# Soft-MoE dispatch sums as a seventh column of the slot product, and e replicated by TensorE

## The chip, the cores and the metric

The kernel runs on one core of a Trainium2 chip. The metric is device time in microseconds (us) of one execution; lower is better. The engines are TensorE (PE; its weight loads are shown apart as PEld), VectorE (DVE), ScalarE (ACT), GpSimd (POOL) and SyncE (SP), each with its own queue of instructions, taken in order.

## The reference, cut to what matters

Soft-capped attention for 8 batches, 12 heads, 448 tokens, head size 64, and then a soft mixture of experts over all 3584 tokens of 768 features, with 32 slots (8 experts of 4):

```python
scores = cap * np.tanh((q @ k.T) / np.sqrt(64) / cap)      # cap = 30
attn = softmax(scores)
x = (attn @ v)                                             # (3584, 768) after the heads are joined
logits = x @ phi                                           # (3584, 32)
d = np.exp(logits - logits.max(0)); d /= d.sum(0) + 1e-09  # dispatch: over the tokens
slot_input = d.T @ x                                       # (32, 768)
for e in range(8):
    h = np.maximum(slot_input[e] @ w1[e], 0.0)
    slot_out[e] = h @ w2[e]
c = np.exp(logits - logits.max(1)); c /= c.sum(1) + 1e-09  # combine: over the slots
return c @ slot_out
```

So one matrix e = exp(logits) serves twice. Summed over the tokens it is the divisor of the dispatch (one number for each slot); turned over, it is the weight of the combine.

## The kernel before, in words

**Stages.** The attention takes the time up to 245 us, then come the experts on the 32 slots (two layers), then the combine and the stores of 11 MB.

**Attention.** Two pairs of heads make a quad (24 quads Q, 48 pairs pr). A score tile is 128 keys by 448 queries, seven of them to a pair, 336 in all. Six tiles make a chunk j (56 chunks); seven chunks (PER) are a batch b. In these texts k is j modulo 7. For each chunk PE makes the scores in two halves of three tiles (`qk_chunk`, L315, into two PSUM buffers `sc`), ACT takes tanh of each half (`tanh_chunk`, L324), and one chunk later exp (`exp_chunk`, L328). Of 33 chunks some tiles are taken off ACT: `SHARED` says how many (78 in all, one to three of a chunk), and `poly_exp` computes their exp on DVE in eight operations, numbered 0 to 7: L560, L562, L563, L564, L565, L566, L567, L568. Each operation works on all the tiles that were taken of the chunk at once. Two chunks after a pair's last tile PE multiplies with v (`pv_first`, `pv_tail`, `pv_rest`, L586; a column of ones in `vbd` gives the divisor) and DVE divides (`norm`: reciprocal L593, product `xq` L596). GpSimd copies v into `vbd` (`vcast`, L285), after `pv_rest` has read the old one, and issues the loads of q, k and the weights.

**Turning.** PE transposes q and k of a quad (`transp`, L275) and the attention's result (`x_transp`, L634 and L639), always into one PSUM bank, tag T of pool psT, which has a single buffer; DVE copies it out (L277, L648). The next use of T waits for that copy. T also serves `logits` (L653, L657), `slot_sums`, `e_norm`, `e_transp` and `e_sums`.

**Around e.** For each batch: `logits` fills `lps` with tokens on partitions in four groups of 128 (the last of 64) and 32 slots; `e_exp` has ACT write E (L673); `e_rep` has GpSimd write e4, four copies of E side by side (L679, 128x512); `slot_sums` multiplies x by E on PE (L719, L725) into `slps`, six columns of 32, and DVE adds them to `slacc` (L734); `e_norm` multiplies e4 by a column of ones into one column, the sum over the tokens, four times along the partitions, which DVE adds to `zacc` (L687, L691); `e_transp` turns e4 with four transposes (L698), and DVE copies the result to ET4 or ETl (L699). There the 32 slots stand four times along the partitions, as layer 2 leaves its results.

**Order.** Each engine takes its work in the order in which the loop over j emits it: tanh of the first half, slot m, tanh of the second half, slot e, exp of the chunk before, `pv_first`, slot a, `pv_tail`, `qk_chunk` for the first half of the next chunk, slot b, `pv_rest` (with slot r inside), slot c, `qk_chunk` for its second half, slot d. A slot has a part ahead (`<c`) and one behind (`>c`). The table `WHEN` puts each job of a batch into a slot, counted in chunks from the batch's start: for example `'x1': (8, 'c')`, the transposes of the batch's second quad; `k1` to `k3` and `q1` to `q3` are the transposes of k and q of three quads, `lg`, `ee`, `ss`, `et`, `en`, `es` the steps around e. The table `POLY` puts each DVE operation (chunk, number) into a slot. `FILL`, `LATE` and `spare` place matmuls without use between.

**After the attention.** The last two pairs are worked off by hand (`TAILSEQ`), then the last batch's e, its slot sums and the last column sums (`z_last`, L961 and L965), and `rz`, one over `zacc`, is made; ACT's relu of layer 1 multiplies by it (L1047). During the stores the last two batches' e are turned (`e_transp(B - 1)`, `e_rep(B - 2)`, `e_transp(B - 2)`), with one e4 buffer for both.

Of the kernel before, what the change touches and what calls it, by code (L numbers as in the profile page):

```python
# [9 lines left out]
F32 = mybir.dt.float32  # L10
# [8 lines left out]
P = 128  # L19
HP = 64  # L20
# [17 lines left out]
def kernel(  # L38
# [47 lines left out]
    half1 = consts.tile([P, 1], BF16, name="half1")  # L86
    pool.memset(half1, 0.0)
    pool.memset(half1[0:HP, :], 1.0)
# [6 lines left out]
    slacc = consts.tile([P, NJ, NS], F32, name="slacc")  # L95
    consts.tile([P, 192], BF16, name="pad")
# [233 lines left out]
    def exp_chunk(j):  # L330
# [11 lines left out]
            (3, '>c'): ((3, 3),),  # L342
            (3, '>d'): ((3, 4),),
            (4, '>a'): ((3, 5), (3, 6), (3, 7), (4, 0)),
            (4, '>c'): ((4, 1),),
            (4, '>d'): ((4, 2),),
            (5, 'e'): ((4, 3),),
            (5, '>b'): ((4, 4),),
            (5, '<c'): ((4, 5),),
# [7 lines left out]
            (7, '<c'): ((7, 2),),  # L357
            (7, '>c'): ((7, 3),),
            (7, '>d'): ((7, 4),),
            (8, '>b'): ((7, 5),),  # L360
            (8, '<c'): ((7, 6),),
            (9, 'e'): ((9, 0),),
            (9, '>a'): ((7, 7),),
# [5 lines left out]
            (10, '>d'): ((9, 6), (9, 7)),  # L369
            (11, '>a'): ((11, 0), (11, 1)),  # L370
            (11, '>b'): ((11, 2),),
# [5 lines left out]
            (12, '>c'): ((12, 2),),  # L377
            (13, '>a'): ((12, 3),),
# [4 lines left out]
            (14, '<c'): ((14, 2),),  # L383
            (14, '>c'): ((14, 3),),
            (14, '>d'): ((14, 4),),
            (15, '>b'): ((14, 5),),
            (15, '<c'): ((14, 6),),
            (16, 'e'): ((16, 0),),
            (16, '>a'): ((14, 7),),
# [5 lines left out]
            (17, '>d'): ((16, 6), (16, 7)),  # L395
            (18, '>a'): ((18, 0), (18, 1)),
            (18, '>b'): ((18, 2),),
# [5 lines left out]
            (19, '>c'): ((19, 2),),  # L403
            (20, '>a'): ((19, 3),),
# [4 lines left out]
            (21, '<c'): ((21, 2),),  # L409
            (21, '>c'): ((21, 3),),  # L410
            (21, '>d'): ((21, 4),),
            (22, '>b'): ((21, 5),),
            (22, '<c'): ((21, 6),),
            (23, 'e'): ((23, 0),),
            (23, '>a'): ((21, 7),),
# [5 lines left out]
            (24, '>d'): ((23, 6), (23, 7)),  # L421
            (25, '>a'): ((25, 0), (25, 1)),
            (25, '>b'): ((25, 2),),
# [5 lines left out]
            (26, '>c'): ((26, 2),),  # L429
            (27, '>a'): ((26, 3),),  # L430
# [24 lines left out]
            (33, '>c'): ((33, 2),),  # L455
            (34, '>a'): ((33, 3),),
# [4 lines left out]
            (35, '<c'): ((35, 2),),  # L461
            (35, '>c'): ((35, 3),),
            (35, '>d'): ((35, 4),),
            (36, '>b'): ((35, 5),),
            (36, '<c'): ((35, 6),),
            (37, 'e'): ((37, 0),),
            (37, '>a'): ((35, 7),),
# [5 lines left out]
            (38, '>d'): ((37, 6), (37, 7)),  # L473
            (39, '>a'): ((39, 0), (39, 1)),
            (39, '>b'): ((39, 2),),
# [5 lines left out]
            (40, '>c'): ((40, 2),),  # L481
            (41, '>a'): ((40, 3),),
# [4 lines left out]
            (42, '<c'): ((42, 2),),  # L487
            (42, '>c'): ((42, 3),),
            (42, '>d'): ((42, 4),),
            (43, '>b'): ((42, 5),),  # L490
            (43, '<c'): ((42, 6),),
            (44, 'e'): ((44, 0),),
            (44, '>a'): ((42, 7),),
# [5 lines left out]
            (45, '>d'): ((44, 6), (44, 7)),  # L499
            (46, '>a'): ((46, 0), (46, 1)),  # L500
            (46, '>b'): ((46, 2),),
            (46, '<c'): ((46, 3),),
            (46, '>d'): ((46, 4), (46, 5)),
            (47, 'e'): ((47, 0), (46, 6)),
# [6 lines left out]
            (48, '>b'): ((47, 6),),  # L511
            (48, '<c'): ((47, 7),),
            (48, '>d'): ((48, 1), (48, 2)),
            (49, '>a'): ((48, 3), (48, 4), (49, 0)),
            (49, '<c'): ((48, 5),),
            (49, '>c'): ((48, 6),),
            (49, '>d'): ((49, 1), (49, 2), (49, 3)),
            (50, '>a'): ((48, 7),),
            (50, '>b'): ((49, 4),),
            (50, '>d'): ((49, 5), (49, 6)),  # L520
            (51, 'e'): ((51, 0),),
            (51, '>a'): ((51, 1), (49, 7), (51, 2)),
            (51, '<c'): ((51, 3),),
            (51, '>d'): ((51, 4),),
            (52, 'e'): ((51, 5),),
            (52, '>a'): ((52, 0),),
            (52, '>b'): ((51, 6), (52, 1)),
            (52, '<c'): ((52, 2),),
            (52, '>c'): ((51, 7),),
# [139 lines left out]
    es, e4s = {}, {}  # L669

    def e_exp(b):
        es[b] = consts.tile([P, NG, NS], BF16, name="E", tag="E", bufs=2)
        act.activation(es[b], lps.pop(b), ACT.Exp)  # L673
        e_rep(b)

    def e_rep(b):

        e4s[b] = consts.tile([P, NG, 4 * NS], BF16, name="e4", tag="e4", bufs=1)
        pool.tensor_copy(e4s[b].rearrange("p g (a s) -> p g a s", a=4),  # L679
                         es[b].unsqueeze(2).to_broadcast([P, NG, 4, NS]))  # L680
# [86 lines left out]
    WHEN = {'k1': (-1, 'd'), 'q1': (0, 'a'), 'v1': (3, 'c'), 'k2': (2, 'b'), 'q2': (2, 'd'), 'v2': (7, 'b'), 'k3': (4, 'b'), 'q3': (5, 'b'), 'v3': (11, 'c'), 'x0': (5, 'a'), 'x1': (8, 'c'), 'x2': (10, 'b'), 'lg': (10, 'd'), 'ee': (11, 'm'), 'ss': (11, 'c'), 'et': (13, 'a'), 'en': (14, 'c'), 'es': (15, 'a')}  # L767

    for b in range(B):
        j, p = b * PER, 6 * b  # L770

        def when(nm):
            return j + WHEN[nm][0], WHEN[nm][1]

# [16 lines left out]
        if b < B - 1:  # L791
            at(*when("lg"), logits, b)
            at(*when("ee"), e_exp, b)
            at(*when("ss"), slot_sums, b)
            if b < B - 2:
                at(*when("et"), e_transp, b)
                at(*when("en"), e_norm, b)
            if b % 2:
                at(*when("es"), e_sums, b // 2)
# [155 lines left out]
    zl = bank([P, 1], name="zps")  # L955

    def z_last(b):
        for g in range(NG):
            n = P if g < NF else HP
            if b < bl:  # L960
                pe.matmul(zl, e4s[b][0:n, g, :], ones[0:n, 0:1], start=(g == 0), stop=False,  # L961
                          skip_group_check=True)
                continue
            for a in range(4):
                pe.matmul(zl[32 * a:32 * a + NS, :], es[b][:, g, :],  # L965
                          ones[:, 0:1] if g < NF else half1, start=False, stop=(g == NG - 1),
                          skip_group_check=True)
# [11 lines left out]
    z_last(bl - 1)  # L979
# [16 lines left out]
    e_rep(bl)  # L996
    z_last(bl)
# [4 lines left out]
    dve.tensor_tensor(zacc, zl, zacc, op=ALU.add)  # L1002
# [204 lines left out]
```

## Time and profile before

| | us |
|---|---|
| median of three runs (lowest, highest) | 293.06 (292.88, 293.4) |
| the profiled execution, its own time | 293.05 |
| its span, first to last instruction | 291.3 |
| busy: PE, DVE, ACT, POOL | 254.9, 241.9, 256.7, 138.8 |
| ACT's last exp of the attention ends | 245.1 |
| first store of the output is issued | 259.5 |

The mean granted clock of TensorE is 0.978. Times in the views are microseconds from the first instruction, and those called mean or from the trace's rows are of this one execution. A row of the timeline gives the start, the time taken, engine, line, operation, what it writes and reads, shapes, the number of instructions merged into it, and in brackets the engine's idle time before it and who ended that. A row of the waits gives who waited for whom, the sum, how often, and the longest.

### The profile page before, as it was taken

The page shows a single profiled execution, that of the slowest core. Times are in us where ns is not written, and L with a number is a line of the kernel's source. Part 1 is how long each engine was busy: PE and PEld are TensorE (multiplying, and loading weights), DVE is VectorE, ACT ScalarE, POOL GpSimd, SP SyncE. Part 2 cuts the span into 40 slices and gives each one's busy share as a digit, 9 for nine tenths or more (in the row PEclk, how much of TensorE's full clock was granted, in tenths as well). Part 3 has the DMA queues.
Part 4 walks back from the last instruction along what each step waited for, and adds up shares of the span by engine and source line. Part 5 has one row for each costly group of instructions (what it writes and reads, how often), then busy time and mean ns, then how long its engine had stood idle before and what let it go on. Part 6 is the DMA issues. An engine that isn't in the chain of part 4 may idle for free.

```text
span 291.3 us, 10806 instructions
## 1 busy us (share of the span) xinstructions
PE 254.9 (88%) x4728; PEld 172.8 (59%) x4728; DVE 241.9 (83%) x506; ACT 256.7 (88%) x211; POOL 138.8 (48%) x200
## 2 busy tenths in 40 slices
PE   8898789989998999899889998999899899998720
PEld 6655466757675767576657675767576668542400
DVE  3727899999999999999999999999999986247740
ACT  4999999999999999999989999999999997237720
POOL 4492645774666567555745656565553220300000
PEclk9999999999999999999999999999999999999965
DMA  7999999999999999999999999999999467979995
GB/s 242 242 192 205 207 183 218 213 206 217 229 224 181 209 234 231 200 207 230 215 196 199 222 218 201 215 228 226 206 184 228 122 227 254 409 290 377 411 423 234
DMA packets 58478, 68.11 MB, mean 234 GB/s; under 512 B 4160, under 2 KB 54592, under 8 KB 58432
## 3 DMA queue, kind: packets, MB, share of 16 engines
q0 software_dynamic: 42448, 35.31, 78.2%
q1 hardware_dynamic: 15696, 31.89, 31.3%
q8 instruction: 37, 0.61, 0.8%
q10 hardware_dynamic: 288, 0.23, 0.2%
q14 instruction: 9, 0.07, 0.1%
HBM read 91.72 MB, written 19.27 MB: 381 GB/s over the span
## 4 chain that ended last, share of the span: by engine, by line
DVE 47%; PE 33%; ACT 8%; DMA 4%; POOL 2%; issue 2%; DVEq 0%; ACTq 0%
PE pv L586 11%; DVE xq L596 8%; PE sc L315 5%; DVE ex L567 5%; DVE xp L566 4%; DVE xT L648 4%; ACT ex L328 3%; DVE xp L564 3%; DVE xf L562 3%; ACT ex L324 3%; DVE ex L560 3%; DVE ex L568 3%; PE pv L616 3%; DVE xp L563 3%; DVE qT L277 3%; DVE kT L277 2%
## 5 line engine op out<-in xcount | busy, mean ns | idle before, releaser
L324 ACT ACTIVATE ex<-sc 128x1344 f16<-128x1344 f32 (+1 forms) x113 | 142.1, 1318 | 2.5 <-PE sc L315 2.4
L328 ACT ACTIVATE ex<-ex 128x2688 bf16<-128x2688 f16 (+5 forms) x58 | 110.2, 1904 | 0.1
L586 PE MATMUL pv<-vbd,ex 128*128 128x130 bf16 (+1 forms) x1610 | 95.1, 211 | 7.6 <-POOL vbd L285 4.7
L586 PEld LDWEIGHTS <-ex 128*128 128x128 bf16 (+1 forms) x1680 | 75.7, 101 | 36.0 <-PE sc L315 7.7
L315 PE MATMUL sc<-qT,kT 64*64 64x448 bf16 x672 | 70.5, 359 | 1.1 <-ACT ex L324 0.7
L285 POOL CAST vbd<-vraw 64x896 bf16<-64x896 f32 x46 | 44.2, 960 | 45.9 <-PE pv L586 30.2
L596 DVE TENSOR_TENSOR xq<-pv,rec 128x448 bf16<-128x448 f32 x46 | 28.7, 624 | 1.6
L315 PEld LDWEIGHTS <-kT 64*64 64x64 bf16 x672 | 23.4, 105 | 6.6 <-issue 5.1
L293 POOL MEMSET vbd<- 64x1 bf16 x22 | 4.0, 180 | 46.3 <-PE pv L586 46.3
L117 POOL DMA_DIRECT2D w1b<-in_moe_w_dram x32 | 24.9, 781 | 0.0
L566 DVE TENSOR_TENSOR xp<-xp,xf 128x1344 f16<-128x1344 f16 (+2 forms) x33 | 23.6, 715 | 0.9
L564 DVE TENSOR_TENSOR xp<-xp,xf 128x1344 f16<-128x1344 f16 (+2 forms) x33 | 23.9, 723 | 0.2
L567 DVE TENSOR_TENSOR ex<-ex,xp 128x1344 uint16<-128x1344 uint16 (+2 forms) x33 | 23.2, 704 | 0.4
L679 POOL COPY e<-E 128x512 bf16<-128x512 bf16 x9 | 6.2, 693 | 36.4 <-PE eps L698 19.9
L616 PE MATMUL pv<-ones 128*128 128x57 bf16 x474 | 18.6, 188 | 0.0
L185 POOL DMA_DIRECT2D qb<-in_q_dram x22 | 16.8, 765 | 3.1 <-DMA kraw<-in_k_dram 3.1
L277 DVE COPY kT<-kps 128x896 bf16<-128x896 bf16 x23 | 14.2, 617 | 4.5 <-PE kps L275 4.3
L275 PE MATMUL qps<-ident,qb 128*64 128x128 bf16 x308 | 12.8, 222 | 5.4 <-DVE xT L648 5.3
L563 DVE TENSOR_SCALAR xp<-xf 128x1344 f16<-128x1344 uint16 (+2 forms) x33 | 16.6, 504 | 0.2
L275 PEld LDWEIGHTS <-qb 128*64 128x64 bf16 x308 | 10.1, 109 | 10.8 <-issue 10.5
L560 DVE TENSOR_SCALAR ex<-ex 128x1344 uint16<-128x1344 f16 (+2 forms) x33 | 16.4, 498 | 0.0
L616 PEld LDWEIGHTS <-ones 128*128 128x128 bf16 x474 | 16.2, 96 | 0.0
(135 smaller groups left out, 361.8 us busy)
## 6 DMA issues: line engine op xcount, KB each, us to landing
w1b<-in_moe_w_dram POOLq DMA_DIRECT2D x32, 384.0 KB, 8.4
vraw<-in_v_dram SPq DMA_DIRECT2D x44, 224.0 KB, 6.1
w2d<-in_moe_w_dram POOLq DMA_DIRECT2D x21, 384.0 KB, 8.5
w2t<-w2d SPq DMA_DIRECT2D x21, 384.0 KB, 7.0
out_dram<-ob SPq DMA_DIRECT2D x7, 768.0 KB, 8.0
qb<-in_q_dram POOLq DMA_DIRECT2D x22, 224.0 KB, 7.5
kb<-in_k_dram POOLq DMA_DIRECT2D x22, 224.0 KB, 6.0
w2b<-in_moe_w_dram POOLq DMA_DIRECT2D x11, 384.0 KB, 7.5
```

What stands on the lines that cost most here:

```text
L277: dve.tensor_copy(t, ps)
L285: pool.tensor_copy(vbds[Q % 2][r, :, :, c0:c0 + DH], raw[r])
L315: pe.matmul(sc[cs, u, 0:S], qkT["k", Q][r, c, cs], qkT["q", Q][r, :, cs], start=True, stop=True)
L324: act.activation(exs[j][:, half * CS + u0:half * CS + u1, :].bitcast(F16), sc[:, u0:u1, 0:S], ACT.Tanh, scale=qk_scale / cap)
L328: act.activation(exs[j][:, u0:u1, :], exs[j][:, u0:u1, :].bitcast(F16), ACT.Exp, scale=cap)
L563: lambda: dve.tensor_scalar(p, f, c3, c2, ALU.mult, ALU.add),
L564: lambda: dve.tensor_tensor(p, p, f, op=ALU.mult),
L566: lambda: dve.tensor_tensor(p, p, f, op=ALU.mult),
L567: lambda: dve.tensor_tensor(y, y, p, op=ALU.add),
L586: pe.matmul(out_, exs[j][r, u, q0:q0 + (HP if tail else P)], v_, start=(c == 0 and g == gs[0] < NF), stop=(c == NT - 1), skip_group_check= ...
L596: dve.tensor_tensor(xq[Q][:, h, s0:s1, :], pv[:, 0:s1 - s0, 0:DH], rec.to_broadcast([P, s1 - s0, DH]), op=ALU.mult)
L616: pe.matmul(home, ones, ones[:, 0:512 - NT * W], start=False, stop=True, skip_group_check=True)
```

## The change

- `e_rep`, `e_norm` and `z_last` go, with e4 and half1. Nothing is copied by GpSimd for e any more.
- `slot_sums` gets a seventh column of 32 in `slps` and `slacc`: a new `z_mms` multiplies a 128x128 block of ones by E, four matmuls, so that each partition holds the sums of all 32 slots.
- At the end DVE adds the last batch's sums to it (`zsum`), multiplies by the identity read as four blocks of 32 (`zdiag`), and reduces each partition to its own slot's sum (`zacc`).
- `e_transp` does sixteen transposes of E's 32 columns, four for each group, each to 32 other partitions, in place of four of 128 columns of e4.
- `SHARED` takes two tiles of chunk 53 instead of one: 79 in all.
- `WHEN`: q1 goes from slot a to slot b of its chunk, x1 from (8, c) to (8, d), x2 from (10, b) to (10, a); `en` goes.
- `POLY` is written anew from chunk 3 on. Below are the rows of one round (chunks 28 to 34) and those of chunks 53 to 55.

```diff
-    slacc = consts.tile([P, NJ, NS], F32, name="slacc")
-    consts.tile([P, 192], BF16, name="pad")
+    slacc = consts.tile([P, NJ + 1, NS], F32, name="slacc")
+    zsum = consts.tile([P, NS], F32, name="zsum")
+    zdiag = consts.tile([P, 4, NS], F32, name="zdiag")
+    consts.tile([P, 336], BF16, name="pad")
...
             (28, '>b'): ((28, 1),),
-            (28, '<c'): ((28, 2),),
-            (28, '>c'): ((28, 3),),
+            (28, '>c'): ((28, 2), (28, 3)),
             (28, '>d'): ((28, 4),),
             (29, '>b'): ((28, 5),),
-            (29, '<c'): ((28, 6),),
-            (30, 'e'): ((30, 0),),
-            (30, '>a'): ((28, 7),),
+            (29, '>c'): ((28, 6),),
+            (29, '>d'): ((28, 7),),
+            (30, '>a'): ((30, 0),),
...
             (31, '>a'): ((30, 5),),
-            (31, '>d'): ((30, 6), (30, 7)),
-            (32, '>a'): ((32, 0), (32, 1)),
-            (32, '>b'): ((32, 2),),
+            (31, '>d'): ((30, 6),),
+            (32, 'e'): ((32, 0), (30, 7)),
+            (32, '>a'): ((32, 1), (32, 2)),
             (32, '<c'): ((32, 3),),
             (32, '>d'): ((32, 4), (32, 5)),
             (33, 'e'): ((32, 6),),
             (33, '>a'): ((32, 7), (33, 0)),
             (33, '>b'): ((33, 1),),
-            (33, '>c'): ((33, 2),),
-            (34, '>a'): ((33, 3),),
+            (33, '<c'): ((33, 2),),
+            (34, 'e'): ((33, 3),),
             (34, '>b'): ((33, 4), (33, 5)),
...
-            (53, 'e'): ((52, 4), (53, 0), (52, 5)),
-            (53, '>a'): ((52, 6),),
+            (53, 'e'): ((52, 4), (52, 5)),
+            (53, '>a'): ((53, 0), (52, 6)),
             (53, '>b'): ((52, 7), (53, 1)),
             (53, '<c'): ((53, 2), (53, 3)),
-            (53, '>c'): ((53, 4),),
-            (54, '>a'): ((53, 5), (53, 6)),
-            (54, '>c'): ((54, 0), (54, 1), (54, 2)),
-            (54, '>d'): ((53, 7),),
-            (55, 'e'): ((54, 3), (54, 4), (54, 5)),
+            (54, 'e'): ((53, 4),),
+            (54, '>b'): ((53, 5), (53, 6)),
+            (54, '<c'): ((54, 0),),
+            (54, '>c'): ((53, 7), (54, 1), (54, 2), (54, 3)),
+            (55, 'e'): ((54, 4), (54, 5)),
             (55, '>a'): ((54, 6), (54, 7))}
...
         act.activation(es[b], lps.pop(b), ACT.Exp)
-        e_rep(b)
-
-    def e_rep(b):
-
-        e4s[b] = consts.tile([P, NG, 4 * NS], BF16, name="e4", tag="e4", bufs=1)
-        pool.tensor_copy(e4s[b].rearrange("p g (a s) -> p g a s", a=4),
-                         es[b].unsqueeze(2).to_broadcast([P, NG, 4, NS]))
-
-    def e_norm(b):
-
-        ps = psT.tile([P, 1], F32, name="zps", tag="T")
+
+    def z_mms(b, dst, alone=False):
+
         for g in range(NG):
             r = slice(0, P if g < NF else HP)
-            pe.matmul(ps, e4s[b][r, g, :], ones[r, 0:1], start=(g == 0), stop=(g == NG - 1))
-        if b == 0:
-            dve.tensor_copy(zacc, ps)
-        else:
-            dve.tensor_tensor(zacc, ps, zacc, op=ALU.add)
+            pe.matmul(dst, ones[r, :], es[b][r, g, :], start=(alone and g == 0), stop=(g == NG - 1),
+                      skip_group_check=True)
...
         for g in range(NG):
             n = P if g < NF else HP
-            pe.transpose(ps[:, g * P:g * P + n], e4s[b][0:n, g, :], ident[0:n, 0:n])
+            for a in range(0, P, NS):
+                pe.transpose(ps[a:a + NS, g * P:g * P + n], es[b][0:n, g, :], ident[0:n, 0:n])
...
     def slot_sums(b):
-        ps = psT.tile([P, NJ, NS], F32, name="slps", tag="T")
+        ps = psT.tile([P, NJ + 1, NS], F32, name="slps", tag="T")
         slot_mms(b, ps, range(NG), range(NJ))
+        z_mms(b, ps[:, NJ, :])
...
-    e_rep(bl)
-    z_last(bl)
+    z_mms(bl, zl, True)
...
-    dve.tensor_tensor(zacc, zl, zacc, op=ALU.add)
+    dve.tensor_tensor(zsum, zl, slacc[:, NJ, :], op=ALU.add)
+    dve.tensor_tensor(zdiag, ident.rearrange("p (a s) -> p a s", s=NS),
+                      zsum.unsqueeze(1).to_broadcast([P, 4, NS]), op=ALU.mult)
+    dve.tensor_reduce(zacc, zdiag.rearrange("p a s -> p (a s)"), axis=mybir.AxisListType.X, op=ALU.add)
     dve.reciprocal(rz, zacc)
...
             e_transp(B - 1)
-            e_rep(B - 2)
```

More of the change, by code (lines that the diff above doesn't have):

```diff
@@ L341 @@
             (3, 'r'): ((3, 2),),
-            (3, '>c'): ((3, 3),),
+            (3, '<c'): ((3, 3),),
             (3, '>d'): ((3, 4),),
[L344 to L347, printed above, removed]
+            (4, '>a'): ((3, 5), (3, 6), (4, 0)),
+            (4, '>b'): ((3, 7),),
+            (4, '<c'): ((4, 1),),
+            (5, 'e'): ((4, 2), (4, 3)),
             (5, '>b'): ((4, 4),),
-            (5, '<c'): ((4, 5),),
+            (5, 'r'): ((4, 5),),
             (5, '>c'): ((4, 6),),
@@ L356 @@
             (7, '>b'): ((7, 1),),
-            (7, '<c'): ((7, 2),),
-            (7, '>c'): ((7, 3),),
+            (7, '>c'): ((7, 2), (7, 3)),
             (7, '>d'): ((7, 4),),
             (8, '>b'): ((7, 5),),
-            (8, '<c'): ((7, 6),),
-            (9, 'e'): ((9, 0),),
-            (9, '>a'): ((7, 7),),
+            (8, '>c'): ((7, 6),),
+            (8, '>d'): ((7, 7),),
+            (9, '>a'): ((9, 0),),
             (9, '>b'): ((9, 1),),
@@ L368 @@
             (10, '>a'): ((9, 5),),
-            (10, '>d'): ((9, 6), (9, 7)),
-            (11, '>a'): ((11, 0), (11, 1)),
-            (11, '>b'): ((11, 2),),
+            (10, '>d'): ((9, 6),),
+            (11, 'e'): ((11, 0), (9, 7)),
+            (11, '>a'): ((11, 1), (11, 2)),
             (11, '<c'): ((11, 3),),
@@ L382 @@
             (14, '>b'): ((14, 1),),
[L383 to L384 removed]
+            (14, '>c'): ((14, 2), (14, 3)),
             (14, '>d'): ((14, 4),),
             (15, '>b'): ((14, 5),),
[L387 to L389 removed]
+            (15, '>c'): ((14, 6),),
+            (15, '>d'): ((14, 7),),
+            (16, '>a'): ((16, 0),),
             (16, '>b'): ((16, 1),),
@@ L394 @@
             (17, '>a'): ((16, 5),),
-            (17, '>d'): ((16, 6), (16, 7)),
-            (18, '>a'): ((18, 0), (18, 1)),
-            (18, '>b'): ((18, 2),),
+            (17, '>d'): ((16, 6),),
+            (18, 'e'): ((18, 0), (16, 7)),
+            (18, '>a'): ((18, 1), (18, 2)),
             (18, '<c'): ((18, 3),),
@@ L420 @@
             (24, '>a'): ((23, 5),),
-            (24, '>d'): ((23, 6), (23, 7)),
-            (25, '>a'): ((25, 0), (25, 1)),
-            (25, '>b'): ((25, 2),),
+            (24, '>d'): ((23, 6),),
+            (25, 'e'): ((25, 0), (23, 7)),
+            (25, '>a'): ((25, 1), (25, 2)),
             (25, '<c'): ((25, 3),),
@@ L472 @@
             (38, '>a'): ((37, 5),),
-            (38, '>d'): ((37, 6), (37, 7)),
-            (39, '>a'): ((39, 0), (39, 1)),
-            (39, '>b'): ((39, 2),),
+            (38, '>d'): ((37, 6),),
+            (39, 'e'): ((39, 0), (37, 7)),
+            (39, '>a'): ((39, 1), (39, 2)),
             (39, '<c'): ((39, 3),),
@@ L954 @@
            psT.tile([P, 2 * P], BF16, name="xpl", tag="T")]
[L955 to L967, printed above, removed]
+    zl = bank([P, NS], name="zps")
     def x_last(s, copy):
@@ L978 @@
     x_last(0, act.copy)
-    z_last(bl - 1)
     busy(3)
```

90 lines of the change are left out of this document (41 added, 49 removed), and 2 rows, old and new, of the table SHARED.

## The prediction, made before the changed kernel ran

> **What bounds the kernel now.** First the table of stages (columns: busy time of PE, PEld, DVE, ACT and POOL with their instruction counts, granted clock, DMA share, GB/s).
>
> ```profile
> 30.00:60.00 30.00, 26.56 (x538) 18.53 (x538) 28.29 (x58) 30.00 (x24) 18.28 (x25) 1.00 1.15 203
> 150.00:180.00 30.00, 28.05 (x569) 19.76 (x568) 29.12 (x61) 29.11 (x22) 18.41 (x27) 1.00 1.22 211
> 210.00:240.00 30.00, 27.69 (x535) 19.27 (x535) 27.14 (x72) 29.89 (x23) 12.06 (x18) 1.00 0.90 187
> 245.00:250.00 5.00, 5.00 (x120) 3.72 (x121) 2.06 (x9) 1.39 (x5) 1.53 (x2) 1.00 1.01 350
> ```
>
> From 6.7 to 245.1 us ScalarE (ACT) is nearly never idle; VectorE (DVE) is close behind at 29.1 of 30. After 245.1 nothing is ACT's: 46.2 us of slot experts and stores, with DMA near 1.0, start from whatever ends the attention. So I ask how much ACT loses before 245.1, and what holds it up. Busy time hides small losses, since neighbouring ACT rows overlap by 0.1 to 0.2 us; I take start to start. A tanh of three tiles starts 1.171 after the last one, an exp of 6, 5, 4, 3 tiles takes 2.333, 1.960, 1.586, 1.213, an E 0.174. What exceeds these is lost: 3.9 us in all, 0.3 of it before 15 us, which the change does not touch. The rest, 3.6 us, lies in two places of the seven-chunk round (k is the chunk number j modulo 7): 1.41 us before E (k=4; 0.25, 0.35, 0.11, 0.28, 0.42 in batches 1 to 5) and 2.19 us before the second tanh of k=6 or, last, k=5 (0.10, 0.10, 0.07, 1.28, 0.12, 0.20, 0.32). The timeline of ACT shows three of them (start, duration, what was idle before):
>
> ```profile
> 111.74 0.28 ACT L673 ACTIVATE E<-lps 128x128 bf16<-128x128 f32 x1 [0.17 <-PE lps L657]
> 150.79 1.29 ACT L324 ACTIVATE ex<-sc 128x1344 f16<-128x1344 f32 x1 [1.14 <-PE sc L315]
> 200.45 0.28 ACT L673 ACTIVATE E<-lps 128x128 bf16<-128x128 f32 x1 [0.23 <-PE lps L657]
> ```
>
> Both wait for PE, but PE is not the cause. In an ordinary round the timeline reads:
>
> ```profile
> 171.81 0.80 POOL L679 COPY e<-E 128x512 bf16<-128x512 bf16 x1 [1.29 <-ACT E L673]
> 172.05 0.80 DVE L560 TENSOR_SCALAR ex<-ex 128x896 uint16<-128x896 f16 x1
> ...
> 177.42 0.62 DVE L648 COPY xT<-xps 128x896 bf16<-128x896 bf16 x1
> 178.09 0.58 PE L275 MATMUL qps<-ident,qb 128*64 128x128 bf16 x14 [0.77 <-DVE xT L648]
> ```
>
> DVE runs without a gap over 0.05 us from 161.7 to 186.8. Its copy of x0 (L648, k=5) comes 0.6 us after PE had finished the transposes; bank T has one buffer, so q3's transposes wait 0.77 us, then pv_rest, then the scores of k=6, which end 0.04 us before their tanh starts. DVE's lateness at k=5 is what ACT pays for at k=6. At 150.79 it is larger, because two DVE operations sat beside GpSimd's cast:
>
> ```profile
> 143.66 1.19 POOL L285 CAST vbd<-vraw 64x896 bf16<-64x896 f32 x1
> 143.85 1.26 DVE L563 TENSOR_SCALAR xp<-xf 128x896 f16<-128x896 uint16 x1
> ```
>
> L563 of two tiles takes 0.38 where GpSimd is idle.
>
> **The change, part by part.** *Copies of e.* Seven lie in the attention stage, 0.61 us each alone. Beside them DVE is slower: L568 of three tiles takes 0.50 alone and 0.73 on average in the six rows beside a copy; L560 of two tiles 0.39 and 0.80; L564 of one tile 0.38 and 0.80. That is 0.24 to 0.42 per batch, 2.8 us in all, and it falls at k=4, just ahead of the x0 copy. GpSimd's DMA issues can move into the freed place; beside one, L560 of two tiles lost 0.20. So the gain is between 0 and 0.42; I take 0.3. The Trainium skill (SBUF — State Buffer, Who interferes with whom) says that VectorE's two-port operations and GpSimd's hold a shared port pair exclusively, so that the second waits in full; the trace agrees with the row at 172.05, and by that rule the whole 0.42 would be gained, 0.8 us of DVE more over seven batches.
>
> *The old sums.* Four matmuls (0.27 of PE at k=0), one use of T and one DVE add of 0.14 go, in six batches. The new four matmuls have full weights and 32 columns like the 18 of L719 in 0.69 us: 4 x 0.038 = 0.15, now at k=4 ahead of the second scores of k=5, which stand 0.6 ahead of their tanh. The slot add grows from 192 to 224 columns: 0.35 x 32/192 is at most 0.06.
>
> *Transposes of e.* Four of 0.10 to 0.12 become sixteen with 32 columns of weights. Nearest rows: sixteen loads with one-column matmuls in that shape took 0.24 (L965), fourteen half-width transposes 0.58 (L275), so 0.25 to 0.66; I take 0.4 against 0.4 now. They stand in k=6, which has no pv and is padded with junk; the next scores are 0.98 ahead of ACT. The Trainium skill (TensorEngine Tiling, Key Properties) says that a change of tiling mode drains TensorE, which speaks against the new shape. PE's weight loads do show 0.36 of idle after the scores' 64x64 shape, and two such extra gaps would be 0.7; the sum would still not move, by the slacks that follow.
>
> *Moves on PE.* From k=6 to k=2 PE is late by its own work, not by waiting: second scores of k=1 are 0.70 ahead, of k=2 0.15 to 0.32. Here 0.27 goes with the old sums; x1 (0.6) moves behind the second scores of k=2 and q1 (0.58) behind the first of k=1. So even 0.8 more in k=6 leaves 0.2 everywhere. x2 moves ahead of k=4's first scores: it then waits for q2's copy until 167.32 and delays those scores by 0.45 of 1.6, but its own copy on DVE comes one L566 earlier (0.86), so that logits start when the second scores end, 0.3 sooner, and E is no longer late.
>
> *DVE's order.* At k=4 L563 moves ahead of k3's copy, away from the cast that cost 0.88 at 143.85. Under that cast then lie a PSUM copy, the reciprocal and xq, which no cast lengthened by over 0.02.
>
> *Tile 79.* ACT's exp of chunk 53 goes from 1.960 to 1.586, 0.37 less. DVE's eight operations grow from the one-tile row sum 2.74 to the two-tile sum 4.20: 1.45 more. DVE idles 0.25, 0.73 and 0.18 between 233.5 and 238.0, 1.16 in all, and the copy of e beside L564 (0.42) goes. I take the two as level: 0.
>
> *End.* Four matmuls go at 246.4 (PE waits for ACT there), sixteen become four at 248.9 beside the slT adds, which layer 1 waits for anyway. DVE's new multiply and reduce (128x128; the nearest rows are 0.15 to 0.35 each) put rz at about 250.1 instead of 249.6; its first use is at 252.24. The copies at 248.5 and 270.7 have nobody waiting beyond 0.2. So 0; with that cover gone it would be 0.5.
>
> **Sum**, against the profiled execution: span 291.3, time 293.05, which is the median of the runs shown. E's waits give 1.2 of 1.41; the small k=6 waits 0.5 of 0.59; the long one 1.2 of 1.28; the last 0.2 of 0.32; tile 79 nothing. From these 3.1 I take back 0.6: DVE works about 28.85 us per round now and 28.85 - 0.3 - 0.14 + 0.06, about 28.5, later, while ACT without waits needs 28.79 (14 x 1.171 + 3 x 2.333 + 1.586 + 3 x 1.213 + 0.174). With so little between them some 0.1 per round should remain. 293.05 - 2.5 = 290.5.
>
> **Rivals.** *ACT never waits* (chance 0.20): all 3.6 and the 0.37 of tile 79: 289.1. For it: DVE would have 0.3 to spare per round. Against it: one slow DVE operation uses that up. *PE takes over* (0.14): the sixteen transposes and drains cost more than the 0.98 of k=0 and every round gives back about 0.3 in seven: 290.5 + 2.1 = 292.6. For it: the slacks of 0.15 to 0.32 in k=2. Against it: q1, x1 and the old sums leave that stretch. *DVE sets the end* (0.14), the one on the other side: in chunks 53 to 55 the 1.45 us land on the x and xq copies that PE's tail waits for. If PE's transposes come as DVE is ready, the 1.16 of idle time is no cover; and if GpSimd's issues fill the freed places, the rounds gain nothing. Then 293.05 + 1.0 (between 0.3 and 1.45), 294.0. It decides from the point where xq of pair 45 ends after 242.6 less what the rounds gained.
>
> **How the numbers follow.** My forecast has 0.52. Measurement tells 0.2%, about 0.6 us, from no change: 292.5 to 293.6. The forecast and the first rival are faster, and a little of the second (0.04): 0.76. Same: the rest of the second, 0.10. Slower: 0.14. The range reaches from the first rival's 289.1 less 0.2 up to 293.2, over the second and its doubts; it leaves out the slower rival and the ends.
>
> **What would show it.** Right: no POOL row at L679; L560 and L568 at k=4 back at 0.39 and 0.50; PE's wait of qps for xT below 0.5 instead of 0.77; E starting 1.17 after its tanh; ACT's last exp ending near 242.6 instead of 245.1; the 46.2 after it unchanged. Wrong: ACT waits for sc at k=0 to k=2 (PE took over), xq of pair 45 later against ACT's last exp than now (DVE sets the end), or a longer stretch after the last exp. A single DVE operation of over 1 us beside a cast, as at 143.85, would also spoil it.

## The result, and the profile after

The changed kernel takes **290.72 us** (median of 22 runs, 289.8 to 294.21), the kernel before 293.01 beside it (22 runs, 292.6 to 295.52): a ratio of 0.9926, with an interval of 0.9903 to 0.995, or 2.2 us less. The forecast was 290.5.

The first profiled execution of the changed kernel took 293.29 us, mostly because TensorE's clock came up 8 us late in it, which is told in the last section; so the profile read here is that of a second execution of the same kernel (290.34 us, span 288.6), and the first is shown only where it says so.

The first part of the page, after (busy time, share of the span, instructions):

```profile
PE 253.2 (88%) x4812; PEld 172.0 (60%) x4812; DVE 239.5 (83%) x502; ACT 255.4 (89%) x211; POOL 134.7 (47%) x189
```

GpSimd has 4.1 us less than before, DVE 2.4 less, although DVE now does a 79th tile. The table of stages of the same execution, with the columns of the one that the prediction shows:

```profile
30.00:60.00 30.00, 26.66 (x545) 18.89 (x545) 28.16 (x59) 30.00 (x24) 18.10 (x24) 1.00 1.17 208
150.00:180.00 30.00, 28.06 (x578) 19.46 (x573) 29.00 (x58) 30.00 (x24) 18.03 (x26) 1.00 1.25 214
210.00:240.00 30.00, 27.50 (x558) 20.18 (x553) 27.28 (x74) 30.00 (x24) 9.29 (x14) 1.00 0.87 188
245.00:250.00 5.00, 5.00 (x107) 3.02 (x108) 1.74 (x8) 0.71 (x3) 1.81 (x1) 1.00 1.03 406
```

ACT is at 30.00 in all three stages of the attention; from 150 to 180 it was at 29.11. DVE is hardly less busy (29.00 against 29.12): its relief shows as an earlier start of what follows, not as idle time. ACT's timeline, the rows that answer to the three shown before:

```profile
110.99 0.71 ACT L665 ACTIVATE E<-lps 128x128 bf16<-128x128 f32 x1
198.11 0.34 ACT L665 ACTIVATE E<-lps 128x128 bf16<-128x128 f32 x1
207.44 1.29 ACT L323 ACTIVATE ex<-sc 128x1344 f16<-128x1344 f32 x1 [0.35 <-PE sc L314]
```

The E rows have no bracket any more: ACT is not idle before them (110.99 is 1.17 after the start of the tanh ahead, as in a row without loss). The row at 207.44 (second tanh of k=6, batch 6) is the largest wait that is left after 22 us, 0.53 from start to start. The whole account, by the prediction's measure (start to start beyond the pitches of tanh, exp and E, after 22 us):

| | before | after |
|---|---|---|
| ACT's first tanh starts | 6.72 | 6.87 |
| waits before E | 1.41 | 0.07 |
| waits for scores | 2.19 | 1.14 |
| ACT's last exp ends | 245.08 | 242.49 |
| from there to the end of the span | 46.20 | 46.07 |

The attention, from the first tanh to the end of the last exp, is 238.36 before and 235.62 after: 2.74 less, of which 2.39 are waits and 0.37 the exp of the 79th tile.

### The profile page after: what moved, and what is told of

Its sections match the earlier page's. It is cut to its first block, busy times and chain, and to the rows that moved or that the text cites. A ratio compares the mean times of both kernels' runs of the same rounds, so it can differ in the third digit from the quotient of the medians.

```text
span 291.5 us, 10965 instructions
## 1 busy us (share of the span) xinstructions
PE 256.1 (88%) x4812; PEld 173.3 (59%) x4812; DVE 239.7 (82%) x502; ACT 256.2 (88%) x211; POOL 134.7 (46%) x189
## 4 chain that ended last, share of the span: by engine, by line
DVE 41%; PE 37%; issue 8%; POOL 6%; DMA 3%; ACT 1%; DVEq 0%; ACTq 0%
PE pv L578 11%; DVE xq L588 8%; PE sc L314 7%; DVE xT L640 4%; DVE ex L559 4%; DVE xp L558 4%; DVE xp L556 3%; PE junk L811 3%; DVE qT L276 3%; DVE ex L560 2%; POOL vbd L284 2%; DVE xf L554 2%; DVE ex L552 2%; DVE rec L585 2%; PE so_ps L1040 2%
## 5 line engine op out<-in xcount | busy, mean ns | idle before, releaser
L314 PE MATMUL sc<-qT,kT 64*64 64x448 bf16 x672 | 73.0, 365 | 0.4 <-DVE qT L276 0.4
L284 POOL CAST vbd<-vraw 64x896 bf16<-64x896 f32 x46 | 45.7, 994 | 56.3 <-issue 25.6
L314 PEld LDWEIGHTS <-kT 64*64 64x64 bf16 x672 | 24.0, 106 | 6.3 <-issue 4.9
L116 POOL DMA_DIRECT2D w1b<-in_moe_w_dram x32 | 25.5, 797 | 0.0
L559 DVE TENSOR_TENSOR ex<-ex,xp 128x1344 uint16<-128x1344 uint16 (+2 forms) x33 | 24.1, 730 | 0.3
L276 DVE COPY qT<-qps 128x896 bf16<-128x896 bf16 x23 | 14.3, 621 | 3.1 <-PE qps L274 3.0
L184 POOL DMA_DIRECT2D kb<-in_k_dram x22 | 16.2, 735 | 0.5 <-PE kps L274 0.5
L560 DVE TENSOR_SCALAR ex<-ex 128x1344 uint16<-128x1344 uint16 (+2 forms) x33 | 16.1, 488 | 0.1
L555 DVE TENSOR_SCALAR xp<-xf 128x1344 f16<-128x1344 uint16 (+2 forms) x33 | 15.8, 479 | 0.3
```

Of the source, the lines that this page charges most:

```text
L184: pool.dma_start(out=t, in_=quad_ap(nm, Q))
L276: dve.tensor_copy(t, ps)
L284: pool.tensor_copy(vbds[Q % 2][r, :, :, c0:c0 + DH], raw[r])
L314: pe.matmul(sc[cs, u, 0:S], qkT["k", Q][r, c, cs], qkT["q", Q][r, :, cs], start=True, stop=True)
L559: lambda: dve.tensor_tensor(y, y, p, op=ALU.add),
```

## The experiments

Twelve runs were made: ten other kernels, and both kernels of the change once more. In each table row below, "E" and "scores" are ACT's waits after 22 us, and "attention" goes from the first tanh to the end of the last exp, all of one profiled execution; "time" is the median of 6 to 12 timed runs (of three in the first row), and the ratio is to the kernel before on the same chip (293.34, 293.24 or 293.47 there).

| kernel | E | scores | attention | tail | time | ratio, interval |
|---|---|---|---|---|---|---|
| before, as in the prediction | 1.41 | 2.19 | 238.36 | 46.20 | 293.06 | |
| before, once more | 1.84 | 2.20 | 238.67 | 46.18 | 293.13 | 0.9982 [0.9954, 1.001] |
| changed kernel | 0.07 | 1.14 | 235.62 | 46.07 | 290.39 | 0.989 [0.9842, 0.9938] |
| structure alone | 1.33 | 1.42 | 237.50 | 46.42 | 292.19 | 0.998 [0.9942, 1.0019] |
| order alone | 0.24 | 3.56 | 239.94 | 46.01 | 292.3 | 0.9968 [0.9931, 1.0005] |
| before, no copies | 1.60 | 0.83 | 237.15 | 46.41 | 291.83 | 0.9947 [0.9914, 0.998] |
| changed, copies back | 0.24 | 2.56 | 237.07 | 46.41 | 291.69 | 0.9956 [0.9916, 0.9995] |
| changed, 78 tiles | 0.26 | 1.62 | 236.62 | 46.38 | 291.52 | 0.9932 [0.9893, 0.9971] |
| changed, x2 back | 1.67 | 1.62 | 237.60 | 45.97 | 292.44 | 0.9978 [0.9946, 1.0011] |
| changed, no column sums | 0.04 | 1.35 | 235.65 | 46.00 | 290.6 | 0.99 [0.9859, 0.9941] |
| changed, L563 back | 0.10 | 1.69 | 236.10 | 45.58 | 290.18 | 0.9897 [0.9855, 0.994] |
| changed, q1 and x1 back | 0.21 | 2.05 | 238.28 | 46.76 | 290.7 | 0.991 [0.9879, 0.994] |
| changed, issues moved | 0.33 | 1.77 | 236.44 | 45.85 | 290.9 | 0.9933 [0.9896, 0.997] |

The profiled executions of "order alone" and "q1 and x1 back" had the late clock too; it costs the attention 1.7 us before 22 us, so their "attention" is not to be compared, their waits after 22 us are. Two executions of one kernel differ by 0.4 to 0.5 in the sum of these waits (3.60 and 4.04 before; 1.66 and 1.21 in the two profiles of the changed kernel), so smaller differences between rows are not read.

**The changed kernel once more**, with no edit.

> The changed kernel once more, unchanged, for a second profile. Its first profiled execution took 293.29 us while the median is 290.72, and loses 2.6 us before 22 us (first tanh at 7.60 instead of 6.72 us, 1.5 us of waits of the next tanhs), where the change alters nothing. Theory A, that this start is a chance of single executions: the new profile shows the first tanh near 6.7 us and about 290.5 us in all. Theory B, that the change slows the start for good: again 7.6 us and 293. Either way the waits of ACT after 22 us should again be about 1.7 us, none of them over 0.1 before E.

It gave 290.39 (289.76 to 292.89): the first profile was the untypical one. All readings of "after" above are from this run.

**Structure alone, and order alone.** The one has the seventh column, z_mms, the sixteen transposes and no copies, with the old tables; the other has the copies and the old sums with the new tables.

```diff
 # structure alone: the changed kernel with SHARED, POLY and WHEN of before
-    WHEN = {... 'q1': (0, 'b'), ... 'x1': (8, 'd'), 'x2': (10, 'a'), ...}
+    WHEN = {... 'q1': (0, 'a'), ... 'x1': (8, 'c'), 'x2': (10, 'b'), ...}
 # order alone: the kernel before with SHARED, POLY and WHEN of after, and
+    WHEN = {... 'en': (14, 'c'), ...}
```

> The new way of summing and replicating e, with the order (POLY, WHEN but for en) and the 78 tiles of before. Theory A, GpSimd's copies were what made DVE late: about 1.2 us of the 2.3 come from here, 291.8 us. Theory B, the copies' place is taken by GpSimd's DMA issues and the gain is the new order's: 292.8 us or more, with E's waits of 0.1 to 0.4 us at k=4 still there and the k=6 waits larger than before, because the column sums now stand ahead of the second scores of k=5.

> The old way of summing and replicating e (GpSimd's copies, e_norm at its old place), with the new order (POLY, q1, x1, x2) and 79 tiles. Theory A: x2 ahead of the first scores takes away E's waits (1.3 us) but DVE stays late beside the copies, 291.9 us. Theory B: the order does it all, 290.7 us, with no long wait at k=6. Theory C, the order only pays when the copies are gone: 293.0 us or more.

Each half alone gives about 1 us (292.19 and 292.3 against 293.34), and both intervals reach past 1; together they give 2.95 on that chip and 2.2 in the main measurement. Whether that is more than the sum of the halves, the intervals do not settle. The profiles show where each half stops. The structure alone cuts the waits for scores and leaves those before E (1.33). The order alone does the reverse; its profiled execution is the slowest of its twelve, so its waits may be larger than usual. The waits of ACT that its view lists show it (engine, line, waited for: sum, number, longest):

```profile
ACT ex L324 <- PE sc L315: 5.4, 9, 2.0
```

In the kernel before the same line reads 2.4 in two waits, 1.2 of them at the start; here 3.3 fall before 22 us, by the late clock, and 2.1 in five waits after it, where before has 1.1 in one. They fall at k=5 and k=6, and DVE stands behind them: ahead of the slot sums PE waits 2.5 us, in five rounds, for DVE's copy of k, where the kernel before and the changed one have 0.4 in one round. "Changed, copies back" below has the same order beside copies, with the seventh column; its waits for scores are 2.56 and its time is 1.5 below the kernel before. So the order does pay beside copies there, and the 3.56 here is the reading of one execution.

**Copies taken out of the kernel before, and put back into the changed one.**

```diff
 # before, no copies
     def e_rep(b):
+        if 0 < b < B - 1:
+            e4s[b] = e4s[0]
+            return
 # changed, copies back: at the end of e_exp, into a tile that nothing reads
+        pool.tensor_copy(e4.rearrange("p (g a s) -> p g a s", g=NG, a=4),
+                         es[b].unsqueeze(2).to_broadcast([P, NG, 4, NS]))
```

> The kernel before, with GpSimd's copies left out for batches 1 to 6 (e_norm and e_transp then read batch 0's e4, so the divisor and the combine weights of these batches are left out of the result). Theory A, each copy costs DVE 0.24 to 0.42 us that ACT pays for at k=6: 292.0 us, L560 of two tiles back at 0.39. Theory B, a DMA issue of GpSimd moves into the place: 292.8 to 293.0, with DVE operations beside L121 and L185 longer instead.

> The changed kernel with GpSimd's copy of E added again in each of the seven batches of the attention (written to a tile that nobody reads; DVE's last product of 128x128 takes part of that tile afterwards). Theory A, DVE's lateness by the copies is what the new structure takes away: waits of ACT after 22 us grow from 1.2 us to about 2.5, 291.5 us. Theory B, the copies cost nothing with the new order: 290.4 us.

Without copies the kernel before gets 1.5 us faster (291.83 against 293.34) and its waits for scores fall from 2.19 to 0.83; putting them back into the changed kernel costs 1.3 (291.69 against 290.39, two chips, so only roughly), with the waits up from 1.21 to 2.80. Both say that the copies are worth about 1.4 us, in the old order as in the new, with an interval of about 1 us to either side of each.

**78 tiles, and x2 back.**

```diff
 # 78 tiles
-              53: (2, 0),
+              53: (1, 0),
 # x2 back
-    'x2': (10, 'a')
+    'x2': (10, 'b')
```

> The changed kernel with one tile of chunk 53 on DVE instead of two, in the same slots. Theory A, ACT sets the end, as its last exp ends 2.6 us earlier and the 46.1 us after it are as before: 290.4 + 0.37 = 290.8 us. Theory B (the prediction's term of zero), DVE's 1.45 us more take back what ACT gains: 290.4 us. Theory C, DVE sets the end: below 290.2.

> The changed kernel with x2's transposes at (10, b) as before, behind the first scores of k=4. Theory A, x2's place alone makes E late: E's waits of 0.1 to 0.4 us come back in five batches, 1.3 us in all, 291.5 us. Theory B, ACT's waits only move between E and k=6 because DVE is the bound: E waits again, the waits at k=6 shrink by as much, 290.4 to 290.7 us.

With 78 tiles the attention is 1.00 longer (0.67 of it waits, the rest, 0.33, about the 0.37 of one tile's exp), and the tail is 0.3 longer, not shorter: DVE does not set the end with 79. With x2 in its old slot the waits before E are back, as the E rows of its ACT timeline say:

```profile
111.60 0.28 ACT L665 ACTIVATE E<-lps 128x128 bf16<-128x128 f32 x1 [0.16 <-PE lps L649]
...
199.49 0.28 ACT L665 ACTIVATE E<-lps 128x128 bf16<-128x128 f32 x1 [0.27 <-PE lps L649]
```

That is 1.67 before E against 0.07, and the attention is 1.98 longer, against 1.45 with the copies back: by these profiles the one letter in `WHEN` is worth rather more than all the copies, once those are gone.

**No column sums.**

```diff
-        z_mms(b, ps[:, NJ, :])
+        if b == 0:
+            z_mms(b, ps[:, NJ, :])
 ...
-            dve.tensor_tensor(slacc, ps, slacc, op=ALU.add)
+            dve.tensor_tensor(slacc[:, 0:NJ, :], ps[:, 0:NJ, :], slacc[:, 0:NJ, :], op=ALU.add)
```

> The changed kernel with the new matmuls for the column sums left out after batch 0, and six columns added instead of seven (the divisor misses batches 1 to 6). Theory A, these four matmuls stand ahead of the second scores of k=5 and are what keeps the waits at k=5 and k=6 alive (1.2 us after 22 us): those waits fall below 0.5 us, 289.7 us. Theory B, the waits come from DVE's x0 copy: unchanged, 290.3 us.

The attention is 235.65 against 235.62: leaving out the four matmuls at k=4 gains nothing. It does free PE (how much is told with PE's terms below), but the freed time turned into a longer wait for DVE's copy of x0, in the waits of PE of this kernel and, below it, of the changed one:

```profile
PE qps L274 <- DVE xT L640: 4.2, 7, 1.0
```

```profile
PE qps L274 <- DVE xT L640: 2.8, 7, 0.6
```

**The kernel before once more, and L563 back in the changed one.** The first asks whether the one long wait at 150.79 is an accident of one execution, the second whether the moved L563 is what removed it.

```diff
 # L563 back, for j = 11, 18, 25, 32, 39
-            (32, '>a'): ((32, 1), (32, 2)),
+            (32, '>a'): ((32, 1),),
+            (32, '>b'): ((32, 2),),
```

> The kernel before, for a second profile. The first one holds one long wait (1.28 us at 150.79) that I put down to L563 beside GpSimd's cast, and a second such pair at 228.8 (0.77 longer). Theory A, the pair is the order's fault and recurs: again waits of 3.6 us after 22 us, with DVE operations over 0.45 us longer beside L285. Theory B, it is a chance of single executions: about 2.3 us of waits, and a shorter span by as much than 291.3, unless other waits take its place.

> The changed kernel with operation 2 (L563) of the k=4 chunks 11, 18, 25, 32, 39 behind k3's copy again, as before. Theory A (the prediction), it then meets the cast of v and is up to 0.88 us longer in single rounds, and k=6 waits for it: 291.0 us or more. Theory B, no collision, since the cast waits for pv_rest: 290.4 us, and the earlier slps would even take away 0.1 us of waits at k=5.

It is no accident. In the second execution of the kernel before the timeline has the same rows at the same place, 0.18 later:

```profile
141.31 0.61 POOL L679 COPY e<-E 128x512 bf16<-128x512 bf16 x1 [0.83 <-ACT E L673]
142.60 1.49 POOL L121 DMA_DIRECT2D w2d<-in_moe_w_dram  x2
143.83 1.19 POOL L285 CAST vbd<-vraw 64x896 bf16<-64x896 f32 x1
144.03 1.26 DVE L563 TENSOR_SCALAR xp<-xf 128x896 f16<-128x896 uint16 x1
...
150.97 1.29 ACT L324 ACTIVATE ex<-sc 128x1344 f16<-128x1344 f32 x1 [1.15 <-PE sc L315]
```

GpSimd was busy from the copy up to the cast, with the load of k and two loads of weights between; DVE lost 0.37, 0.20 and 0.36 in three operations beside them. The cast starts 0.20 ahead of L563, which then ends 0.27 after it. With the copies gone L563 starts first. First the kernel before without copies, then the changed kernel with L563 back (there the same operation is called L560):

```profile
143.39 0.38 DVE L563 TENSOR_SCALAR xp<-xf 128x896 f16<-128x896 uint16 x1
143.45 1.11 POOL L285 CAST vbd<-vraw 64x896 bf16<-64x896 f32 x1 [1.16 <-PE pv L586]
```

```profile
142.40 0.38 DVE L560 TENSOR_SCALAR xp<-xf 128x896 f16<-128x896 uint16 x1
142.70 0.93 POOL L284 CAST vbd<-vraw 64x896 bf16<-64x896 f32 x1 [0.97 <-PE pv L583]
```

L563 starts first by 0.06 and by 0.30, and takes its 0.38; in the closer case it is the cast that is longer (1.11 against 0.93). In the kernel before without copies the cast stands where it stood, 4.60 after the start of the last x copy of DVE (4.59 with copies: 139.24 to 143.83), and L563 0.25 nearer to it (4.54 for 4.79), because DVE lost 0.66 in the three operations instead of 0.93. So a quarter of a microsecond of DVE's time ends a loss of 0.88. The kernel with L563 in its old place is as fast as the changed one (290.18 against 290.39 on the other chip): with the copies gone, the move of L563 is not needed, and no row of this operation in the k=4 chunks is lengthened beside a cast there. With the copies there, the move parts the pair as well, but only half of the wait goes: in "order alone" the same operation lies beside a weight load and not beside the cast (0.35 longer), and the long wait of 1.28 is 0.64. The Trainium skill (SBUF — State Buffer, Who interferes with whom) says that whichever of a two-port VectorE operation and a GpSimd operation issues first holds the shared port pair to its end, and the other waits in full; the rows agree: 0.20 behind the cast cost 0.88, 0.06 ahead of it cost nothing.

A second pair of this kind is not parted by the copies' removal. At 228.80 in the kernel before, operation 1 of one tile (L562) lies 0.21 behind a cast and takes 1.03, 0.77 longer than elsewhere. The same row stands in its second execution, in "before, no copies" and in "structure alone"; of the kernels with the new `POLY` only "x2 back" has it (0.66 longer). In these five profiles the last wait at k=5 is 0.32 to 0.91, in the other nine it is at most 0.15. That the pair causes that wait was not tested by itself.

**q1 and x1 back, and weight loads moved.** Which of the other moves matter, and whether the DMA issues beside k=4's operations are what is left.

```diff
 # q1 and x1 back
-    'q1': (0, 'b'), 'x1': (8, 'd')
+    'q1': (0, 'a'), 'x1': (8, 'c')
 # issues moved: weight loads that fall on k=4 go three chunks back
-        at(1 + n * (NCH - 5) // len(wjobs), "b", *job)
+        jw = 1 + n * (NCH - 5) // len(wjobs)
+        at(jw - 3 * (jw % PER == 4), "b", *job)
```

> The changed kernel with q1 at (0, a) and x1 at (8, c) as before. Theory A (the prediction's slacks: second scores of k=2 0.15 to 0.32 ahead, 0.27 more without the old sums, and sixteen transposes that take no longer than four): nothing waits, 290.4 us, with the second scores of k=2 0.3 to 0.6 ahead instead of 0.67 to 0.85. Theory B, PE is late from k=6 to k=2: waits of sc appear at k=1 or k=2, 291.5 us.

> The changed kernel with GpSimd's weight loads of the k=4 chunks issued three chunks earlier (k=1), where DVE has idle time. Beside them L560 and L562 at k=4 are 0.2 to 0.3 us longer, ahead of the x0 copy. Theory A, DVE's lateness at k=4 is what is left of ACT's waits: these fall from 1.2 us after 22 us to about 0.5, 289.8 us. Theory B, the same lengthening at k=1 costs as much, or the k loads move into the place: 290.4 us or more.

Neither moves the time by more than the intervals: 290.7 and 290.9. With q1 and x1 in their old slots one wait of 0.29 at k=2 appears (at 192.80), the place that the prediction named as the tightest; its waits sum to 2.26, which the late start may have added to. With the issues moved the waits are 2.10 instead of 1.21, so they did not fall as the first theory had it. No kernel here is clearly faster than the changed one.

## Why the prediction was right, point by point

The total and its place are right: ACT's last exp ends at 242.49 (forecast 242.6) and the tail is 46.07 (46.2 unchanged). The terms against what they measured, against the profiled execution of before:

| term | forecast | measured |
|---|---|---|
| waits before E | -1.2 | -1.34 |
| long wait at k=6 | -1.2 | -1.28 |
| last wait, k=5 | -0.2 | -0.32 |
| small waits at k=6 | -0.5 | +0.55 |
| taken back | +0.6 | |
| tile 79 | 0 | -0.37 |
| sum | -2.5 | -2.76 |

**E's waits: right, and shown.** x2 back brings them back, 1.67. In "order alone" they go too, but its one profile has 1.4 more of waits for scores in their place; "changed, copies back" has 0.4 more.

**The long wait: right in size, the cure one of two.** That it came from L563 beside the cast is borne out by the same pair in two executions. The step named L563's new place as the cure. Alone it is half of one (0.64 left); the copies' removal alone is the better one (0.22 left at that place without copies), and with it L563 may stay where it was.

**The small waits of k=6: the step that failed.** They were to fall by 0.5, because DVE's copy of x0 would come earlier. What is left for k=5 and k=6 together went from 0.59 to 1.14 (0.13 of it new waits at k=5), a miss of 1.05. The 0.6 taken back for just this lack of room, a flat allowance, covers a little over half of it. That the sum still came out is luck for the rest: the three terms above gave 0.34 more than forecast, and tile 79, put at nothing, gave 0.37.

PE's wait for that copy did fall, from 5.3 us to 2.8 in the seven waits, but mostly because PE comes later, not because the copy comes earlier: it is 5.3 in "before, no copies" as well, and 4.2 in the changed kernel without column sums. Counted from the start of E in the first six batches (before, without the collision of batch 4), PE ends the transposes of x0 after 5.6 to 5.7 us before and 5.8 to 6.4 in the changed kernel, and DVE starts the copy after 6.3 to 6.4 before and 5.9 to 6.8 now. In the timeline of an ordinary round of the changed kernel:

```profile
140.46 1.48 POOL L120 DMA_DIRECT2D w2d<-in_moe_w_dram  x2
140.48 0.39 DVE L552 TENSOR_SCALAR ex<-ex 128x896 uint16<-128x896 f16 x1
140.79 0.76 DVE L560 TENSOR_SCALAR ex<-ex 128x1344 uint16<-128x1344 uint16 x1
141.47 0.69 DVE L554 TENSOR_SCALAR xf<-ex 128x896 uint16<-128x896 uint16 x1
...
146.36 0.62 DVE L640 COPY xT<-xps 128x896 bf16<-128x896 bf16 x1
147.04 0.58 PE L274 MATMUL qps<-ident,qb 128*64 128x128 bf16 x14 [0.21 <-DVE xT L640]
```

PE waits 0.21 here instead of 0.77. But ACT reaches E earlier, by the waits it no longer has, and counted from there the copy is where it was: the second scores of k=6 still end 0.04 before their tanh in most rounds. The largest of these waits, 0.53 at 207.44, shows where it starts:

```profile
204.02 0.62 DVE L559 TENSOR_TENSOR ex<-ex,xp 128x896 uint16<-128x896 uint16 x1
204.57 0.38 DVE L552 TENSOR_SCALAR ex<-ex 128x896 uint16<-128x896 f16 x1
204.87 0.62 DVE L640 COPY xT<-xps 128x896 bf16<-128x896 bf16 x1
205.54 0.58 PE L274 MATMUL qps<-ident,qb 128*64 128x128 bf16 x14 [0.64 <-DVE xT L640]
```

The transposes of x0 end at about 204.4 on PE, and DVE has two operations of the poly exp before its copy. A wait in this place is there in all nine kernels with the new `POLY` (0.34 to 0.93) and is 0.18 to 0.21 in the three with the old one, so the table at this batch is the likely cause. That an operation moved behind the copy would remove it was not tried, and why it is 0.5 here and 0.1 to 0.2 in the other batches stays open. Neither leaving out the column sums nor moving the DMA issues made the sum of the waits smaller.

**Copies: 0.3 per batch was right.** Summed over the rows in which a DVE operation was over 0.15 us longer than its shortest, the loss is 8.2 us in the profile of before, 8.5 in its second one, 4.0 after. Of the 4.2 that went, 1.5 are the two pairs beside a cast, which leaves 2.7, or 0.38 a batch. "Structure alone" gives the price in the old order: all DVE operations up to the last exp last 245.0 us in sum before and 242.0 there; 0.9 of that is the old sums, and the wider slot add takes 0.2, so 2.3 are left, 0.33 a batch. Not all of the 0.42 came: GpSimd's DMA issues moved into the place, as the rows at 140.46 to 141.47 show. Operation 0 of two tiles (L552) is back at its 0.39, but operation 7 of three tiles (L560 there) takes 0.76 and not the forecast 0.50, and operation 1 (L554) 0.69 instead of 0.38. With each such row put to the GpSimd row that it overlaps most, the 2.7 us beside copies are gone, and what lies beside the weight loads grew from 0.9 to 1.9.

**PE's terms: the transposes right, the column sums too small.** The sixteen transposes take 0.49, the four before them 0.47. The four matmuls of the column sums were put at 0.15 and cost 0.40: from the start of the slot sums to the end of the scores behind them, PE needs 1.28 us in every round of the kernel before, 1.68 in the changed one, and 1.28 again in "no column sums". The rows of PE show how, before and after:

```profile
174.06 0.60 PE L719 MATMUL slps<-E,xq 128*128 128x32 bf16 x18
174.72 0.38 PE L315 MATMUL sc<-qT,kT 64*64 64x448 bf16 x2
```

```profile
172.16 0.60 PE L701 MATMUL slps<-E,xq 128*128 128x32 bf16 x18
172.99 0.36 PE L671 MATMUL slps<-E,ones 128*128 128x32 bf16 x4
173.28 0.57 PE L314 MATMUL sc<-qT,kT 64*64 64x448 bf16 x6
```

The scores start 0.66 after the slot sums before, beside the last of these, and 1.12 after them now. Their lead over their tanh, the second of k=5, was 0.61 to 0.69 in batches 1 to 6, the collision aside; it is 0.04 to 0.55 now, and 0.26 to 0.82 without the column sums. So the slack that the prediction counted on there is nearly used up. That costs the changed kernel only the 0.13 of new waits at k=5, since k=6 waits for DVE anyway; in "structure alone" the wait at this place in the last batch is 0.91, where both kernels with the old sums and the old order have 0.32.

"PE takes over" falls: scores of k=1 and k=2 are now 1.09 and 0.67 to 0.85 ahead of their tanh (0.70 and 0.15 to 0.32 before). The transposes in the new shape show no gap beyond those of the kernel before; how much of the 0.40 of the column sums is a change of shape was not separated.

**Tile 79: mis-sized.** ACT's 0.37 are gained and DVE's 1.45 cost nothing, since DVE has idle time (0.43 ahead of 231.1 and 0.58 ahead of 234.1 are left) and no copy there; taking the tile back costs 1.00 of attention in one profile, 1.1 in the medians with overlapping intervals. "DVE sets the end" falls with it.

**The end: right.** The tail lies between 45.6 and 46.8 in all kernels, 46.20 before and 46.07 after. The divisor `rz` is done at 247.98, 1.76 ahead of its first use.

**Rivals.** "ACT never waits" was the next best: 1.2 us of waits are left, which is nearly all that lies between 290.4 and its 289.1.

## What to carry to other kernels

Where two engines run level, test a part both by taking it out of the old kernel and by putting it back into the new one: the copies came to 1.5 and 1.3 us that way, while two halves of about 1 us each against 2.9 together looked like more than a sum and are not settled by their intervals. Before a move of an instruction is credited with ending a conflict, look at which of the two starts first and by how much: here 0.20 us behind a cast cost 0.88, 0.06 ahead of it nothing, so that a few tenths saved anywhere ahead of the pair parted it as well as the move did, while a second pair, elsewhere, stayed until the order changed. A wait that hangs on a thin slack comes back in another place when the waiting engine gets earlier too; forecast it as a lump of slack, not as separate terms, and count from the engine that is the bound: a wait of PE that gets shorter may only mean that PE comes later.

## What was not expected of the hardware

TensorE's granted clock reaches full speed at different times of the start. In eleven of the fourteen profiled executions it does so at 3.91 to 6.02 us, in three at 13.32 to 13.54 (the first profile of the changed kernel, order alone, q1 and x1 back). Until then matmuls of 128 columns follow each other in 107 ns instead of 55. The start of the kernel before, and of the changed kernel's first profile:

```profile
5.93 1.36 PE L315 MATMUL sc<-qT,kT 64*64 64x448 bf16 x12
6.72 2.54 ACT L324 ACTIVATE ex<-sc 128x448 f16<-128x448 f32 x3 [1.23 <-PE sc L315]
```

```profile
6.23 2.45 PE L314 MATMUL sc<-qT,kT 64*64 64x448 bf16 x12
7.60 2.54 ACT L323 ACTIVATE ex<-sc 128x448 f16<-128x448 f32 x3 [1.99 <-PE sc L314]
...
13.27 1.29 ACT L323 ACTIVATE ex<-sc 128x1344 f16<-128x1344 f32 x1 [0.66 <-PE sc L314]
```

The first scores take 2.45 instead of 1.36, the first tanh starts 0.7 to 0.9 later (7.60 against 6.87 and 6.72), and ACT then waits for scores at 13.27, 14.78 and 21.36 us (0.77, 0.34 and 0.56 from start to start). Together that is about 2.5 us, nearly as much as the whole change. The stretches at full clock last 266.24, 269.65, 273.07 or 276.48 us, multiples of 3.413. The Trainium skill (TensorE: Matmul & The Clock Gate, Part 1: The HAM clock gate) says that the clock is granted by the activity in free-running windows of 3.4 us; the steps agree, and a window that lies badly against the first 4 us of matmuls would explain the late grant. No run here moved that start, so this stays an explanation and not a finding. For a comparison it means that a single profile can be off by about 2.5 us within its first 22 us, so the first tanh and the clock of the first 15 us are to be looked at before two profiles are compared.
